# One pipeline step of a fused attention and two-layer kernel, its TensorE order written anew

## The chip, the cores and the metric

The kernel runs on one core of a Trainium2 chip. Its time is the device time of one execution in microseconds (us); of several executions the median counts. Before the change three executions took 552.87, 554.39 and 555.17 us, so the median is 554.39 us.

A core has five engines that run their own queues in order and meet only through semaphores: TensorE (PE in the profile, with PEld for its weight loads), VectorE (DVE), ScalarE (ACT), GpSimd (POOL) and SyncE (SP, which here issues the transfers).

## The reference, cut to what matters

```python
# q, k, v: batch 2, heads 8, sequence 768, head size 64; n_global 8, n_local 96
scores = q @ k.T / 8 - slope[h] * dist            # local band and a few global columns are kept
a = softmax(scores);  x = a @ v                   # x: 1536 tokens x 512
h = x @ w_in                                      # 1536 x 1024
s = h * softmax(h)
ln = (s - mean(s)) / sqrt(var(s) + 1e-6) * g_ln
y = ln @ w_out                                    # 1536 x 512
xn = y / sqrt(mean(y*y) + 1e-6) * rms_g
g, val = xn @ w_gate, xn @ w_val                  # 512 -> 1536 each
out = (g * sigmoid(g) * val) @ w_out2             # 1536 x 512
```

Everything is in 32 bit. The large matmuls are made of three products each: an operand is split into a high part and a low part (`hi`, `lo`), and hi·hi, hi·lo and lo·hi are added up in PSUM.

## The kernel before, in words

The 1536 tokens are cut into 12 units of 128 tokens. A unit goes through the first three layers (attention, `w_in` with its softmax and layer norm, `w_out` with its root mean square); that is phase 1. Phase 2, some 60% of the time, takes the normalised units in groups of four through the gated layer.

Phase 1 is a software pipeline. Its first part is an order written out by hand (`START`), which also converts the weights. From the fifth unit on, `slot(u)` runs once for each u from 4 to 10: seven slots. Six of them hold the full set of work; the last has no scores left to do. One slot works on five units at once:

- `up` for unit u: 2 x 12 matmuls of 512 columns into the banks `h` (line 475), then a maximum on DVE (line 483).
- `p_t` and `attend` for unit u+1: the softmax rows are transposed on PE (line 318, bank `t`), copied to SBUF by ACT or DVE (lines 326 and 328), and multiplied with v (line 340, bank `x`). Each of the four steps does two heads. `x_evac` then splits the result into `xhi` (ACT) and `xlo` (DVE, line 358), which the next slot's `up` reads.
- `scores` for unit u+2, in two halves of four heads: the matmul (line 265, 64 rows of the array for each head), the maximum with the bias on DVE (line 280), the exponential on ACT (line 291), and the division on POOL (line 302).
- `soln` for unit u: the softmax of h on ACT and DVE (lines 497 to 528), which frees the two `h` banks when its products (line 507) are done.
- `ln_t` for unit u-2: the result is transposed on PE (line 542) and split into `lhi` (ACT) and `llo` (DVE, line 226).
- `down` for unit u-3, in four parts of 6 matmuls into the single bank `d` (line 560). After the last part `rms` squares it on ACT (line 573), takes the power on POOL (line 577) and scales it on DVE (line 579, `xn`), which frees the bank.
- `xn_t` for unit u-4: its `xn` is transposed on PE (line 589) and split into `xgh` (ACT) and `xgl` (DVE).

The order on PE in a slot is the order of the calls in `slot`. The orders of ACT, DVE, POOL and SP in the slots are set by the framework's own scheduler, which works from the same calls; so a new order of calls moves these queues too. PSUM has eight banks: two each for `h`, `s` and `t`, one each for `x` and `d`. A tile that asks for a bank waits until its former tile has been read for the last time. The `t` banks are shared in turn by `p_t`, `ln_t` and `xn_t`.

Of the kernel before, what the change touches and what calls it, by code (L numbers as in the profile page):

```python
# [25 lines left out]
NU = B * NB  # L26
# [3 lines left out]
KF = FF // P  # L30
# [12 lines left out]
LEAD = 1  # L43
LAG = 2
DLAG = 3
# [50 lines left out]
w_lo 14 vector, s_exp 5 0, so_mean 2, s_norm 5 0, s_max 5 1, ln_t 1 0  # L96
ln_t 1 1, so_mul 3 0, so_mean 3, s_exp 5 1, s_norm 5 1, w_lo 15 vector
so_var 3, down 0 2, w_mul 12 none, w_mul 14 none, down 0 3, so_var 2"""
N_START = 4
ORDER = [b * NB + j for j in range(NB) for b in range(B)]  # L100
EPS = 1.0e-6
# [19 lines left out]
class Kernel:  # L121
# [127 lines left out]
        )  # L249
        self.v[i] = t  # L250

    def scores(self, u, hh):
        self.s_mm(u, hh)
        self.s_max(u, hh)
        self.s_exp(u, hh)
        self.s_norm(u, hh)
# [488 lines left out]
    def phase1(self):  # L745
# [4 lines left out]
        with self.tc.manual_schedule(engines={E.PE}):  # L750
            for u in range(N_START, NU - LEAD):
                self.slot(u)

    def slot(self, u):

        a = u + LEAD
        s = a + 1
        if s < NU:
            self.load_unit(s)
        if u < NU:  # L760
            self.up(u, 0)
        if a < NU:
            self.p_t(a, 0)
            self.p_t(a, 1)
        if u < NU:
            self.up(u, 1)
        if a < NU:
            self.attend(a, 0)
            self.attend(a, 1)
            self.p_t(a, 2)  # L770
            self.p_t(a, 3)
        if s < NU:
            self.scores(s, 0)
        else:
            self.ln_t(u - LAG, 0, "s")
        if a < NU:
            self.attend(a, 2)
            self.attend(a, 3)
            self.x_evac(a)
        if s < NU:  # L780
            self.ln_t(u - LAG, 0)
        self.ln_t(u - LAG, 1)
        if s < NU:
            self.scores(s, 1)
        if u < NU:
            self.soln(u)
        if u > DLAG:
            self.xn_t(u - DLAG - 1, "t" if s < NU else "s")
        if u >= DLAG:
            for part in range(KF // 2):  # L790
                self.down(u - DLAG, part)

    def phase2(self, w1x, w2x):
        tc, E = self.tc, mybir.EngineType
# [310 lines left out]
```

## Time and profile before

| what | value |
|---|---|
| median of three executions | 554.39 us |
| the profiled execution | 552.96 us, of it 551.1 us between its first and last instruction (the span) |
| PE busy | 526.2 us (95% of the span) |
| PEld, DVE, ACT, POOL busy | 77%, 61%, 43%, 33% |
| mean granted clock of TensorE | 0.991 of full speed |
| chain of work that ended last | PE 78%, DVE 14%, POOL 3%, ACT 2% of the span |

How to read it: a busy share says how much of the span an engine worked, not what the others waited for. Matmuls overlap, so the time from the start of one to the start of the next (the step) is what a matmul costs; the profile's duration of one is longer. So the pace of PE is read from the starts of its instructions, not from its busy time. What is in brackets at the end of a row is idle time of the engine and who ended it.

### The profile page before, as it was taken

To read this page: it belongs to the slowest core of one execution; us is meant where nothing else is said; L and a number is where in the kernel's file an instruction comes from. 1 tells how busy PE (TensorE), PEld (TensorE's weight loads), DVE (VectorE), ACT (ScalarE), POOL (GpSimd) and SP (SyncE) were. 2 spreads that over 40 slices of the span, in tenths; PEclk is the share of its full clock that TensorE was granted. 3 is DMA by queue.
4 is the path that set the end of the run, shared out by engine and by line. 5 is a ranking of instruction groups with operands and counts; after the bars stand their busy time and mean duration, and the time that the engine had idled before them with its cause. 6 is when DMAs were issued, how large, how long until landed. Compare 5 with 4: busy or idle time off the path is not lost.

```text
span 551.1 us, 7636 instructions
## 1 busy us (share of the span) xinstructions
PE 526.2 (95%) x2736; PEld 424.2 (77%) x2736; DVE 338.5 (61%) x797; ACT 235.2 (43%) x557; POOL 179.2 (33%) x207
## 2 busy tenths in 40 slices
PE   4789989999999999999999999999999999999995
PEld 3456767778777888888888888888888888888883
DVE  6989999775577567984725556565654574331312
ACT  5678767664574465643422333422222223111110
POOL 4885253312330331323611332532332232211010
PEclk9979999999999999999999999999999999999999
DMA  8764612330231021340402122222111211020202
GB/s 289 252 231 153 243 47 68 96 96 24 73 97 39 1 77 41 114 152 1 152 2 76 40 76 96 96 78 76 54 62 39 75 40 39 0 77 0 77 0 83
DMA packets 16669, 45.92 MB, mean 83 GB/s; under 512 B 1904, under 2 KB 2928, under 8 KB 16624
## 3 DMA queue, kind: packets, MB, share of 16 engines
q1 hardware_dynamic: 16624, 45.36, 24.3%
q8 instruction: 23, 0.38, 0.3%
q14 instruction: 22, 0.18, 0.1%
HBM read 42.21 MB, written 3.15 MB: 82 GB/s over the span
## 4 chain that ended last, share of the span: by engine, by line
PE 78%; DVE 14%; POOL 3%; ACT 2%; DMA 1%; issue 1%; SPq 0%; POOLq 0%; DVEq 0%; ACTq 0%
PE gv L634 36%; PE op L658 17%; PE yp L560 11%; PE hp L475 9%; DVE p L280 3%; POOL p L302 2%; DVE e L507 2%; PE tp L318 2%; PE xps L340 1%; DVE hst L483 1%; PE tp L589 1%; DVE xlo L358 1%; DVE llo L226 1%; DMA wsh<-in_w_in 1%; DVE pT L328 1%
## 5 line engine op out<-in xcount | busy, mean ns | idle before, releaser
L634 PE MATMUL gv<-xgh,w2hi 128*128 128x512 f32 x288 | 112.2, 390 | 0.0
L634 PE MATMUL gv<-xgl,w2hi 128*128 128x512 f32 x288 | 112.1, 389 | 0.0
L634 PE MATMUL gv<-xgh,w2lo 128*128 128x512 f32 x288 | 112.0, 389 | 0.0
L226 POOL TENSOR_TENSOR alo<-th,ahi 128x512 fp32r<-128x512 f32 x36 | 46.7, 1297 | 199.7 <-ACT ahi L225 199.7
L302 POOL TENSOR_SCALAR p<-p,ast 128x256 f32<-128x256 f32 (+1 forms) x96 | 57.8, 619 | 103.0 <-DVE ast L284 67.5
L475 PE MATMUL hp<-win,xhi 128*128 128x512 f32 x192 | 66.0, 407 | 0.7 <-ACT xhi L220 0.7
L225 ACT ACTIVATE ahi<-th 128x512 fp32r<-128x512 f32 x36 | 22.8, 632 | 98.2 <-DVE th L622 98.2
L620 ACT ACTIVATE th<-gv 128x512 f32<-128x512 f32 x36 | 21.5, 596 | 98.5 <-PE gv L634 98.5
L634 PEld LDWEIGHTS gv<-xgh,w2lo 128*128 128x128 f32 x288 | 54.1, 188 | 11.3
L634 PEld LDWEIGHTS gv<-xgh,w2hi 128*128 128x128 f32 x288 | 54.1, 188 | 11.1
L634 PEld LDWEIGHTS gv<-xgl,w2hi 128*128 128x128 f32 x288 | 54.1, 188 | 11.1
L560 PE MATMUL yp<-wout,lhi 128*128 128x512 f32 x192 | 60.9, 398 | 0.3 <-DVE wout L458 0.3
L621 DVE SCALAR_TENSOR_TENSOR th<-th,gv 128x512 f32<-128x512 f32 x36 | 24.7, 687 | 58.1 <-ACT th L620 58.1
L226 POOL TENSOR_TENSOR w2lo<-wc,w2hi 128x512 fp32r<-128x512 f32 x36 | 49.7, 1384 | 29.6 <-ACT w2hi L225 29.6
L658 PE MATMUL op<-w2hi,alo 128*128 128x512 f32 x144 | 56.0, 389 | 0.0
L658 PE MATMUL op<-w2lo,ahi 128*128 128x512 f32 x144 | 56.0, 389 | 0.0
L658 PE MATMUL op<-w2hi,ahi 128*128 128x512 f32 x144 | 56.0, 389 | 0.0
L622 DVE SCALAR_TENSOR_TENSOR th<-th,gv 128x512 f32<-128x512 f32 x36 | 24.7, 687 | 42.9 <-PE gv L634 42.7
L291 ACT ACTIVATE p<-p,ast 128x256 f32<-128x256 f32 (+1 forms) x96 | 45.9, 480 | 7.1 <-DVE ast L284 3.9
L392 DVE TENSOR_SCALAR wc<-wc 128x512 uint32<-128x512 uint32 x36 | 22.4, 626 | 39.9 <-ACT wc L220 39.8
L475 PEld LDWEIGHTS hp<-win,xhi 128*128 128x128 f32 x192 | 37.1, 193 | 9.3 <-ACT xhi L220 1.4
L394 DVE SCALAR_TENSOR_TENSOR wc<-ws,wc 128x512 uint32<-128x512 uint32 x36 | 40.4, 1123 | 1.1
(118 smaller groups left out, 921.5 us busy)
## 6 DMA issues: line engine op xcount, KB each, us to landing
ws<-in_w SPq DMA_DIRECT2D x36, 512.0 KB, 3.3
qk<-in_qk SPq DMA_DIRECT2D x20, 384.0 KB, 4.0
v<-in_v SPq DMA_DIRECT2D x10, 512.0 KB, 4.1
out_dram<-acc SPq DMA_DIRECT2D x12, 256.0 KB, 2.4
wsh<-in_w_in SPq DMA_DIRECT2D x4, 512.0 KB, 5.4
wsl<-in_w_in SPq DMA_DIRECT2D x4, 512.0 KB, 6.0
wsh<-in_w_out SPq DMA_DIRECT2D x4, 512.0 KB, 4.0
wsl<-in_w_out SPq DMA_DIRECT2D x4, 512.0 KB, 4.8
```

The lines of the kernel that those rows point to most:

```text
L225: self.nc.scalar.activation(out=hi, in_=src, func=AF.Copy)
L226: lo_eng.tensor_tensor(lo, src, f32(hi), ALU.subtract)
L291: self.nc.scalar.activation(out=pt[:, i, 0:W], in_=pt[:, i, 0:W], func=AF.Exp, scale=0.125, bias=st[:, 1, i:i + 1], accum_out=st[:, 2, i:i ...
L302: nc.gpsimd.tensor_scalar(pt[:, i, 0:W], pt[:, i, 0:W], st[:, 3, i:i + 1], 0.0, ALU.mult, ALU.add)
L392: nc.vector.tensor_scalar(w, w, 3, None, ALU.logical_shift_left)
L394: nc.vector.scalar_tensor_tensor(out=w, in0=low, scalar=29, in1=w, op0=ALU.logical_shift_right, op1=ALU.bitwise_or)
L475: nc.tensor.matmul(hp, a[:, k, :], self.win[w][:, k, c], start=(n == 0), stop=(n == len(mms) - 1))
L560: nc.tensor.matmul(yp, a[:, k, :], self.wout[w][:, k, :], start=(k == 0 and n == 0), stop=(k == KF - 1 and n == 2),)
L621: nc.vector.scalar_tensor_tensor(out=a, in0=a, scalar=1.0, in1=g, op0=ALU.add, op1=ALU.mult)
L622: nc.vector.scalar_tensor_tensor(out=a, in0=a, scalar=0.5, in1=v, op0=ALU.mult, op1=ALU.mult)
L634: nc.tensor.matmul(pp, w[:, c], a[:, k, :], start=(n == 0), stop=(n == 3 * KD - 1))
L658: nc.tensor.matmul(self.ops[t], a[:, c], w[:, c0], start=(first and n == 0), stop=(last and n == 2))
```

## The change

`slot` is written as a table, `SLOT`, of 23 steps, and a short loop that calls them. The same steps run on the same units; what differs is their order, and the PSUM bank of the second half of the scores, which is now one of the `h` banks (`scores 1 h`) instead of `s`.

```diff
+SLOT = """\
+up 0, load_unit, p_t 0, p_t 1, up 1, p_t 2, p_t 3, down 0, attend 0, attend 2, attend 1, soln, attend 3,
+ln_t 0 t, scores 0 s, scores 1 h, down 1, down 2, x_evac, xn_t, ln_t 1, down 3"""
...
-    def scores(self, u, hh):
-        self.s_mm(u, hh)
+    def scores(self, u, hh, bank="s"):
+        self.s_mm(u, hh, bank)
...
-        a = u + LEAD
-        s = a + 1
-        if s < NU:
-            self.load_unit(s)
-        if u < NU:
-            self.up(u, 0)
-        if a < NU:
-            self.p_t(a, 0)
-            self.p_t(a, 1)
-        if u < NU:
-            self.up(u, 1)
-        if a < NU:
-            self.attend(a, 0)
-            self.attend(a, 1)
-            self.p_t(a, 2)
-            self.p_t(a, 3)
-        if s < NU:
-            self.scores(s, 0)
-        else:
-            self.ln_t(u - LAG, 0, "s")
-        if a < NU:
-            self.attend(a, 2)
-            self.attend(a, 3)
-            self.x_evac(a)
-        if s < NU:
-            self.ln_t(u - LAG, 0)
-        self.ln_t(u - LAG, 1)
-        if s < NU:
-            self.scores(s, 1)
-        if u < NU:
-            self.soln(u)
-        if u > DLAG:
-            self.xn_t(u - DLAG - 1, "t" if s < NU else "s")
-        if u >= DLAG:
-            for part in range(KF // 2):
-                self.down(u - DLAG, part)
+        unit = dict(up_mm=u, up_max=u, soln=u, p_t=u + LEAD, attend=u + LEAD, x_evac=u + LEAD,
+                    load_unit=u + LEAD + 1, scores=u + LEAD + 1, ln_t=u - LAG, down=u - DLAG,
+                    up=u, xn_t=u - DLAG - 1)
+        for step in SLOT.split(","):
+            name, *args = step.split()
+            i = unit[name]
+            if i < NU and (i >= 0 or name not in ("down", "xn_t")):
+                if u + LEAD + 1 >= NU and (name == "xn_t" or step.split()[:2] == ["ln_t", "0"]):
+                    args = args[:name == "ln_t"] + ["s"]
+                getattr(self, name)(i, *(int(x) if x.isdigit() else x for x in args))
```

On PE, in a full slot, from the last matmuls of the second `up` on. Names: hp is `up`, xps the product with v, tp a transpose (of p, e or xn), sA and sB the scores, yp is `down`. Before:

```order
L475 MATMUL hp<-win_131,xhi 128x512 x4
L340 MATMUL xps<-pT,v 64x128 x8
L318 MATMUL tp<-ident,p 128x128 x8
L265 MATMUL sA<-qk 128x256
L265 MATMUL sB<-qk 128x256
...
L340 MATMUL xps<-pT,v 64x128 x8
L542 MATMUL tp<-ident,e 128x128 x8
L265 MATMUL sA<-qk 128x256
...
L589 MATMUL tp<-ident,xn 128x128 x4
L560 MATMUL yp<-wout_132,lhi 128x512
```

After the last row shown stand the other 23 matmuls of `down`, and then the next slot. The same place of the changed kernel, where all lines are 3 higher:

```order
L478 MATMUL hp<-win_131,xhi 128x512 x4
L321 MATMUL tp<-ident,p 128x128 x8
L563 MATMUL yp<-wout_132,lhi 128x512
...
L343 MATMUL xps<-pT,v 64x128 x16
L545 MATMUL tp<-ident,e 128x128 x4
L268 MATMUL sA<-qk 128x256
L268 MATMUL sB<-qk 128x256
...
L563 MATMUL yp<-wout_132,lhi 128x512
...
L592 MATMUL tp<-ident,xn 128x128 x4
L545 MATMUL tp<-ident,e 128x128 x4
```

The two runs of products with v are one run of 16, the two runs of scores are one of 8 (each counts twice in the trace, where a 32 bit matmul shows as two), the transposes of p stand between `up` and the first 6 matmuls of `down`, and the rest of `down` is cut into runs of 12 and 6.

On ACT, one full slot, from the square of the last `down` (sq<-yp) on: pT copies, the exponentials of h (e<-hp), of the scores (p<-p), the square of the centred e (sq<-e), and the high parts xhi, lhi, xgh. Before:

```order
L573 ACTIVATE sq,rst<-yp 128x512
L326 ACTIVATE pT<-tp 128x512
L500 ACTIVATE e,hst<-hp,hst 128x512
...
L220 ACTIVATE xhi<-xps 128x512
L225 ACTIVATE lhi<-tp 128x512 x2
L291 ACTIVATE p,ast<-p,ast 128x256 x4
L225 ACTIVATE xgh_1252<-tp 128x4x128
L291 ACTIVATE p,ast<-p,ast 128x256 x4
L524 ACTIVATE sq,hst<-e 128x1024
```

and in the changed kernel:

```order
L576 ACTIVATE sq,rst<-yp 128x512
L329 ACTIVATE pT<-tp 128x512 x2
L503 ACTIVATE e,hst<-hp,hst 128x512 x2
L527 ACTIVATE sq,hst<-e 128x1024
L228 ACTIVATE lhi<-tp 128x512
L223 ACTIVATE xhi<-xps 128x512
L294 ACTIVATE p,ast<-p,ast 128x256 x8
L228 ACTIVATE xgh_1264<-tp 128x4x128
L228 ACTIVATE lhi<-tp 128x512
```

The square of e moved from the end of the slot to a place ahead of `lhi` and of all score exponentials, the eight score exponentials stand in one run, and `xgh` and the second `lhi` stand behind them.

## Rows read from the trace of the kernel before

**Rows 1.** Stretches: length, then busy us of PE, PEld, DVE, ACT, POOL, clock.

```profile
86.67:106.94 20.27, 19.46 (x127) 15.24 (x126) 18.10 (x67) 14.82 (x42) 7.54 (x15) 1.00 0.23 73
106.94:201.43 94.49, 93.77 (x621) 75.31 (x620) 61.43 (x216) 52.81 (x150) 23.98 (x46) 1.00 0.19 59
201.43:218.10 16.67, 16.56 (x109) 13.56 (x108) 11.37 (x27) 7.64 (x17) 1.63 (x4) 1.00 0.00 1
218.10:551.10 333.00, 326.31 (x1461) 269.83 (x1459) 170.32 (x239) 98.11 (x175) 98.38 (x77) 1.00 0.19 64
```

**Rows 2.** Timeline of one full slot on PE: start us, us, instruction.

```profile
125.86 0.39 PE L475 MATMUL hp<-win,xhi 128*128 128x512 f32 x1
...
128.59 1.03 PE L318 MATMUL tp<-ident,p 128*128 128x128 f32 x8
129.38 0.48 PE L475 MATMUL hp<-win,xhi 128*128 128x512 f32 x1
...
132.29 1.09 PE L340 MATMUL xps<-pT,v 128*64 128x128 f32 x16
...
134.34 0.48 PE L265 MATMUL sA<-qk 64*128 64x256 f32 x1
...
134.66 0.38 PE L265 MATMUL sA<-qk 64*128 64x256 f32 x1
...
134.87 0.38 PE L265 MATMUL sA<-qk 64*128 64x256 f32 x1
...
135.40 1.09 PE L340 MATMUL xps<-pT,v 128*64 128x128 f32 x16
136.42 1.09 PE L542 MATMUL tp<-ident,e 128*128 128x128 f32 x8
137.45 0.48 PE L265 MATMUL sA<-qk 64*128 64x256 f32 x1
```

**Rows 3.** Timeline of all engines behind the second scores, first and third slot.

```profile
100.95 0.42 PEld L589 LDWEIGHTS tp<-ident,xn 128*128 128x128 f32 x4 [0.88 <-DVE llo L226]
...
138.79 0.42 PEld L589 LDWEIGHTS tp<-ident,xn 128*128 128x128 f32 x4 [0.54 <-DVE llo L226]
...
139.20 0.71 PE L560 MATMUL yp<-wout,lhi 128*128 128x512 f32 x2
```

**Rows 4.** Timeline on PE in the first part, where 32 products stand together.

```profile
62.17 1.97 PE L340 MATMUL xps<-pT,v 128*64 128x128 f32 x32
64.07 1.09 PE L542 MATMUL tp<-ident,e 128*128 128x128 f32 x8
...
65.84 0.38 PE L265 MATMUL sA<-qk 64*128 64x256 f32 x1
...
66.17 0.49 PE L475 MATMUL hp<-win,xhi 128*128 128x512 f32 x1
```

**Rows 5.** Groups in one full slot, by shape: count, busy us, mean ns, idle before.

```profile
L291 ACT ACTIVATE p<-p,ast 128x256 f32<-128x256 f32 x8 | 4.0, 498 | 0.5 <-DVE hst L525 0.4
L280 DVE CUSTOM_DVE_ANT_0 p<-sB,bias 128x256 f32<-128x256 f32 x4 | 1.7, 418 | 0.0
L500 ACT ACTIVATE e<-hp,hst 128x512 f32<-128x512 f32 x2 | 1.4, 690 | 3.5 <-DVE hst L497 3.5
L226 DVE TENSOR_TENSOR llo<-tp,lhi 128x512 fp32r<-128x512 f32 x2 | 1.3, 680 | 0.0
L524 ACT ACTIVATE sq<-e 128x1024 bf16<-128x1024 f32 x1 | 1.0, 1042 | 0.0
L579 DVE SCALAR_TENSOR_TENSOR xn<-yp,rst,rms_bc 128x512 f32<-128x512 f32 x1 | 0.8, 750 | 0.7 <-POOL rst L577 0.7
```

**Rows 6.** Timeline of POOL in one full slot.

```profile
141.14 2.42 POOL L302 TENSOR_SCALAR p<-p,ast 128x256 f32<-128x256 f32 x4 [13.51 <-DVE ast L284]
143.98 1.84 POOL L302 TENSOR_SCALAR p<-p,ast 128x256 f32<-128x256 f32 x4 [0.43 <-DVE ast L300]
145.99 0.55 POOL L577 TENSOR_TENSOR rst<-rst,neghalf 128x1 f32<-128x1 f32 x1 [0.17 <-DVE rst L574]
```

## The prediction

> **What bounds the kernel now.** I first cut the span into stretches. The six full slots run from 86.67 to 201.43 us; the last five of them take 94.49 us, 18.90 each, and PE is busy in 93.77 of these, at a clock of 1.00 [rows 1]. DVE has 61.43 of work there, ACT 52.81, POOL 23.98, so each has room, and what stands on PE is the time. Behind the slots come 333.00 us with PE busy in 326.31 [rows 1]; a time saved ahead of that stretch is saved at the end, if its start finds the converted weights ready, and nothing in the change alters how many there are to convert.
>
> Then I read PE's timeline of one slot, for the starts of runs and not for durations. Twelve matmuls of `up` take 2.73 us (125.86 to 128.59), .227 each [rows 2]. The other runs cost more than their steps, since each change of kind costs something at its ends: eight transposes take .79 between two runs of `up` (128.59 to 129.38), but 1.03 between products with v and scores (136.42 to 137.45) [rows 2]. Four scores take 1.06 (134.34 to 135.40) the first time and 1.34 the second (137.45 to 138.79), where PE's weight load for `xn_t` waits for `llo` on DVE [rows 2, 3]. That wait is the only one of PE that I see in a slot; the rest is pace.
>
> **The change part by part.** The work on PE is the same, instruction for instruction; I price its new runs from these rows, per full slot.
>
> - The wait. `xn_t` needs a `t` bank that the first `ln_t` held until `llo` was done. In the new order the banks are asked for by four p_t, `ln_t 0`, `xn_t`, `ln_t 1`, so `xn_t` takes the bank of the fourth p_t, copied some eight us before. What is late next is `ln_t 1`, which needs the first `llo`; I put that some two us ahead of its need. Saved: 1.34 - 1.06 = .28.
> - Products with v: 1.02 twice (135.40 to 136.42 [rows 2]) become one run of 32, which the first part of the program has too: 62.17 to 64.07, 1.90 [rows 4]. Saved: .14.
> - The second p_t pair stands between matmuls of 512 columns now: .79 for 1.03. Saved: .24. (1.03 is 132.29 to 134.34 less one run of products.)
> - The second four scores follow the first with the step of .21 (134.66 to 134.87 [rows 2]): .84 for 1.06. Saved: .22. The step from scores to a 512-column matmul is in no full slot; in the first part it took .33 (65.84 to 66.17 [rows 4]), against .32 from scores to products (134.87 + .21 to 135.40). Cost .01; bounds: .1 less, if nothing has to be changed, and .2 more, twice the surplus of the runs above.
> - `down` in three runs of 6, 12 and 6. The run behind `xn_t` takes 139.20 to 144.76 (125.86 + 18.90), 5.56 for 24 x .227 = 5.45, so a run's start costs .11 [rows 2, 3]. Two starts more cost .22. The change to products with v, .07 (129.38 to 132.29 is 2.91: 2.73 + .11 + .07), is paid as before.
> - `ln_t` in halves. One half with `xn_t`, between 512-column runs, costs .79; the other 1.03 less four transposes of .10, .63. Before it was 1.03 and, for `xn_t`, .41 (138.79 to 139.20 [rows 3]). Saved: .02.
>
> Sum: .28 + .14 + .24 + .22 - .01 - .22 + .02 = .67, a slot of 18.23. As a cross-check, the new slot in its order, `up`, p_t, `up`, p_t, `down` 6, products, `ln_t`, scores, `down` 12, transposes, `down` 6: 2.73 + .79 + 2.84 + .79 + 1.54 + 1.90 + .63 + 1.90 + 2.84 + .79 + 1.47 = 18.22.
>
> What must hide. Everything else moves off PE, and its cover is now thinner.
>
> - The borrowed `h` bank: the second scores wait for the second product of `soln`. `up` ends at 6.4 of a slot, and maximum, a small instruction, two exponentials and the product (.68 + .2 + 1.38 + .68 [rows 5]) end near 9.6, or 9.9 with hand-overs; the second scores are due at 12.2. Without that cover each us costs one us a slot, since the whole rest of PE's queue stands behind.
> - The single `d` bank: `down 0` comes at 7.1 now, and not at 13.3 (139.20 - 125.86), and needs `xn` of the `down` before.
> - That `xn` closes a ring without PE. DVE works in order: behind `xn` two maxima of `up` with a copy between them; then exponentials on ACT, products, the mean, the square on ACT that now stands ahead of `lhi`; `llo`; and only behind `llo` the maxima of the scores; then eight exponentials in a row, the last four divisions on POOL, and behind them the power for the next `xn`. Durations [rows 5, 6]: .75 + 3 x .68 + 2 x .69 + .68 + .75 + 1.04 + .69 + .68 + 5 x .42 + 8 x .50 + 1.84 + .55 = 16.5 (where no row has the shape, the nearest of the same engine). Some twelve hand-overs come on top; POOL's rows show .17 and .43 of idle time at two, others overlap. At .05 each the ring takes 17.1 us, at .2 it takes 18.9. I take .1, 17.7: the small waits are nearer to .17 than the rows' .43, and DVE's durations overlap, which a sum of them counts twice. That is half a us under 18.22. Before, the ring had PE in it and `xn` came long before it was asked for.
>
> POOL's prices could move with DVE's. In the slot shown four divisions took 2.42 the first time and 1.84 the second: one of them was .58 longer, while DVE subtracted the mean from SBUF to SBUF [rows 6]. The Trainium skill, page SBUF — State Buffer, section Who interferes with whom, says that GpSimd shares a port pair with VectorE and that a VectorE instruction with at most one SBUF input, outside its two-port modes, does not contend for it. By that rule the new neighbours of the divisions, `xgl` and `llo`, which read one operand from PSUM, cost them nothing, and the mean now runs while POOL is idle. If rather any large DVE instruction stretched a division, the ring would grow by .58 for each.
>
> Total: six full slots x .67 = 4.0; in the first of them the wait was longer by .88 - .54 = .34 [rows 3]; the seventh slot has no scores, keeps about .1 of these savings by price, and up to .7 if its waits go too: I take .5. That is 4.9, rounded to 5. The profiled execution took 552.96 us, so 548.0. It is 1.43 under the median; the same saving from 554.39 gives 549.4, my forecast.
>
> **The rivals.**
>
> - The ring decides a little: hand-overs nearer to .15, a ring of 18.5. Then PE waits .3 in most slots, at a transpose that needs a `t` bank or at `down 0`: 5 - 6 x .3 = 3.2, 551.2. For it: half a us is thin in a sum of twenty terms. Against it: in this trace most of these engines' instructions follow each other at once.
> - The change doesn't do what it says: the cost of a change of kind moves to the new places (start of `down` three times, scores to `down` at the upper bound), and only the waits go. 7 x .28 + .34 = 2.3: 552.1. For it: two of the new changes have no row in a full slot. Against it: the long run of products and the transposes at .79 have theirs.
> - Slower: divisions on POOL stretched by DVE. At 17.7 + .58 k the ring passes the present slot of 18.90 with k = 3; from there the kernel is slower. With k = 3, 19.44, it loses .54 in six slots, 3.2: 557.6; with all eight, 22.3 and 575. For it: the .58 of this trace; against it: the other seven divisions of the slot were not stretched, one of them beside `xgl`.
> - The start of the last stretch finds weights late, since the conversions of the last slot stand elsewhere in ACT's and DVE's queues: one loss of 0 to 3, which leaves 549 to 552.
>
> **How the numbers follow.** Forecast .64; the ring decides a little .16; only the waits .10; slower .06; late weights .04. Under .5% (2.8 us, about what a measurement can tell from no change) lies the border at 551.6. All of the forecast's own range, 547.4 to 550.8 (each full slot between .45 and 1.0), is on the faster side, and most of the first rival and half of late weights: .64 + .11 + .02 = .77. Within .5%: the rest of these and the second rival, .17, of which I give .02 to slower for what I don't see: .15 and .08. The range reaches down to 547.0, where a slot saves nearly 1.1, and up to 552.5, so that it holds the ring's case and the second rival; beyond it are the slower case and parts of the others.
>
> **What the profile after would show.** Full slots of 18.2; one run of products of 1.90; scores to `down` in .3 to .4; no idle time of the weight load at `xn_t`; `xn` done some 5 us into a slot, two before `down 0`. The ring would show as idle time of PE at the first transposes of p behind `llo` or `xgl`, or at `down 0` behind `xn`, and as a second maximum of `up` that starts at once behind the copy and not behind PE. A stretched division shows as over 2 us for four. I am wrong if the slots are as long as before, if PE idles at the borrowed bank behind the products of `soln`, or if the saving is there at 201 us and gone at 260.

## The result, and the profile after

The changed kernel takes 548.98 us (median of 6 runs, 548.07 to 551.18), the kernel before 553.60 beside it (6 runs, 552.01 to 555.17): a ratio of 0.9917, 95% interval 0.9896 to 0.9939. It is faster by 4.6 us, 0.8%; 549.4 was forecast, in 547.0 to 552.5. Its profiled execution took 548.55 us with a span of 546.7, against 552.96 and 551.1.

The table has 22 steps, as many as the slot before had calls. All lines of the code after it are three further down: L592 transposes `xn`, L563 is `down`, L229 makes `llo` and `xgl`, L268 the scores.

The span of after in stretches, with the columns of [rows 1]: first full slot, five more, the seventh, the hand-over to the first `gate_val`, and all behind the slots.

```profile
86.27:105.62 19.35, 19.00 (x128) 15.33 (x126) 16.47 (x63) 13.03 (x37) 4.67 (x10) 1.00 0.21 73
105.62:196.62 91.00, 91.00 (x622) 75.11 (x620) 62.97 (x215) 51.55 (x152) 21.12 (x46) 1.00 0.19 62
196.62:212.70 16.08, 16.08 (x110) 13.54 (x108) 13.18 (x31) 10.57 (x25) 5.05 (x10) 1.00 0.11 34
212.70:238.62 25.92, 24.91 (x128) 20.32 (x126) 23.60 (x46) 14.42 (x30) 8.94 (x8) 1.00 0.41 142
212.70:546.70 334.00, 326.75 (x1461) 269.83 (x1459) 169.96 (x239) 97.01 (x173) 97.52 (x76) 1.00 0.18 62
```

Five full slots take 91.00 us, 18.20 each, and PE is busy in all of it; before it was 94.49 [rows 1], 18.90. The first saves .93, the five 3.49, the seventh .59: 5.0. But the stretch behind the slots has become 1.00 longer with the same work (334.00 for 333.00 [rows 1]), although its last part happened to be .42 shorter. The hand-over alone is where it went: this is the line of the kernel before.

```profile
218.10:242.60 24.51, 24.51 (x127) 20.31 (x126) 21.77 (x41) 15.42 (x32) 9.78 (x9) 1.00 0.39 140
```

From 24.51 to 25.92 is 1.41, and PE idles in 1.01 of it. So the span's -4.4 is made of -5.0 in the slots, +1.4 at the hand-over, and -.40 and -.42 at the two ends, which belong to no part of the change: the first part of the program, unchanged, ended at 86.27 here and at 88.58 in another execution of the same kernel.

PE's timeline of one full slot of after, to be read for the starts of runs, as [rows 2] were.

```profile
126.54 1.03 PE L321 MATMUL tp<-ident,p 128*128 128x128 f32 x8
127.33 0.48 PE L478 MATMUL hp<-win,xhi 128*128 128x512 f32 x1
...
130.16 1.03 PE L321 MATMUL tp<-ident,p 128*128 128x128 f32 x8
130.95 0.71 PE L563 MATMUL yp<-wout,lhi 128*128 128x512 f32 x2
...
132.50 1.97 PE L343 MATMUL xps<-pT,v 128*64 128x128 f32 x32
134.39 0.66 PE L545 MATMUL tp<-ident,e 128*128 128x128 f32 x4
134.98 0.48 PE L268 MATMUL sA<-qk 64*128 64x256 f32 x1
...
136.59 0.38 PE L268 MATMUL sA<-qk 64*128 64x256 f32 x1
...
136.91 0.73 PE L563 MATMUL yp<-wout,lhi 128*128 128x512 f32 x2
...
139.77 0.60 PE L592 MATMUL tp<-ident,xn 128*128 128x128 f32 x4
```

Both pairs of p_t take .79, the 32 products 1.90 (132.50 to 134.39), the eight scores 1.93, the step from the last score to `down` .32, and no row has a wait in brackets: the .54 of [rows 3] is gone. Run by run this is the list of the prediction's cross-check, each within .05.

VectorE in the same slot, at the second maximum of `up` (L486).

```profile
127.73 0.75 DVE L582 SCALAR_TENSOR_TENSOR xn<-yp,rst,rms_bc 128x512 f32<-128x512 f32 x1 [1.00 <-POOL rst L580]
...
130.35 0.69 DVE L486 TENSOR_REDUCE hst<-hp 128x1 f32<-128x512 f32 x1 [0.68 <-PE hp L478]
```

`xn` is written 3.9 to 4.7 us into the slot, 2.5 before `down 0` at 7.13, and the second maximum waits .68 for PE and not behind the copy (.67 or .68 in four of the five slots, .22 in the first): in this order the ring does not decide. Eight divisions on GpSimd follow each other in 3.81 us, .48 each, though `xgl` (125.25) and `llo` (125.86) run beside them: the stretch of .58 of [rows 6] is not there. The port rule that the prediction took from the Trainium skill (SBUF — State Buffer, Who interferes with whom) agrees with that here.

Now the hand-over. PE, ScalarE and VectorE of after, from the time at which unit 11's products of `soln` are done (225.2).

```profile
232.00 0.66 PE L592 MATMUL tp<-ident,xn 128*128 128x128 f32 x4 [0.53 <-DVE xn L582]
...
233.60 0.50 PE L563 MATMUL yp<-wout,llo 128*128 128x512 f32 x1 [0.48 <-DVE llo L229]
```

```profile
225.83 0.67 ACT L223 ACTIVATE wc<-ws 128x512 f32<-128x512 f32 x1 [1.17 <-DMA ws<-in_w]
...
227.65 1.06 ACT L527 ACTIVATE sq<-e 128x1024 bf16<-128x1024 f32 x1 [0.68 <-DVE e L519]
...
228.71 0.65 ACT L223 ACTIVATE wc<-ws 128x512 f32<-128x512 f32 x1
229.26 0.58 ACT L576 ACTIVATE sq<-yp 128x512 bf16<-128x512 f32 x1
```

```profile
226.53 0.43 DVE L395 TENSOR_SCALAR wc<-wc 128x512 uint32<-128x512 uint32 x1 [0.29 <-ACT wc L223]
226.87 0.75 DVE L519 TENSOR_SCALAR e<-e,hst 128x1024 f32<-128x1024 f32 x1
...
231.19 0.75 DVE L582 SCALAR_TENSOR_TENSOR xn<-yp,rst,rms_bc 128x512 f32<-128x512 f32 x1 [0.45 <-POOL rst L580]
231.86 1.08 DVE L401 SCALAR_TENSOR_TENSOR wc<-ws,wc 128x512 uint32<-128x512 uint32 x1
232.87 1.27 DVE L229 TENSOR_TENSOR llo<-tp,lhi 128x512 fp32r<-128x512 f32 x2
```

Read it from PE backwards. The transposes of `xn` (unit 8) wait for `xn`, which waits for the square of `yp` on ScalarE (229.26); `yp` had been done since 225.0. That square stands behind two scalings of weight pieces (`wc<-ws`) and behind unit 11's square, which waited for unit 11's mean on VectorE (226.87). The mean stands in VectorE's queue behind L395 of the sixth piece of the second stage's weights; that waits for ScalarE's scaling, and that for a transfer. It is one piece further on than before: in the changed program the scheduler begins with the conversions 8.6 us ahead of the slots' end, where it was 6.9, and each later piece stands one place nearer to the front. The second wait on PE has the same form: `llo` behind L401 of the next piece.

The late transfer is the smaller part of it. These are unit 11's second maximum and its mean in the kernel before, and then the maximum of after.

```profile
224.84 0.68 DVE L483 TENSOR_REDUCE hst<-hp 128x1 f32<-128x512 f32 x1
...
230.78 0.74 DVE L516 TENSOR_SCALAR e<-e,hst 128x1024 f32<-128x1024 f32 x1
```

```profile
220.55 0.68 DVE L486 TENSOR_REDUCE hst<-hp 128x1 f32<-128x512 f32 x1
```

Counted from the end of the slots (218.10 and 212.70), the mean comes at 14.17 us, where it came at 12.68. Of these 1.49, 1.11 are there already at the maximum (7.85 for 6.74), since VectorE works on the third and fourth pieces ahead of it, for whose transfers nothing waited. The other .38 comes with L395 of the sixth, and its idle time is .29.

### The profile page after: what moved, and what is told of

Its sections match the earlier page's. It is cut to its first block, busy times and chain, and to the rows that moved or that the text cites. A ratio compares the mean times of both kernels' runs of the same rounds, so it can differ in the third digit from the quotient of the medians.

```text
span 546.7 us, 7640 instructions
## 1 busy us (share of the span) xinstructions
PE 523.4 (96%) x2736; PEld 424.3 (78%) x2736; DVE 339.4 (62%) x797; ACT 233.9 (43%) x557; POOL 176.1 (32%) x207
## 4 chain that ended last, share of the span: by engine, by line
PE 82%; DVE 10%; POOL 3%; DMA 1%; ACT 1%; issue 1%; POOLq 0%; ACTq 0%; SPq 0%; DVEq 0%
PE gv L637 36%; PE op L661 18%; PE yp L563 9%; PE hp L478 8%; PE xps L343 3%; PE tp L321 3%; POOL p L305 2%; PE sA L268 2%; DVE p L283 2%; PE tp L545 1%; DMA ws<-in_w 1%; PE tp L592 1%; DVE llo L229 1%; DVE wout L461 1%; DVE e L510 1%
## 5 line engine op out<-in xcount | busy, mean ns | idle before, releaser
L229 POOL TENSOR_TENSOR alo<-th,ahi 128x512 fp32r<-128x512 f32 x36 | 46.7, 1297 | 200.5 <-ACT ahi L228 200.5
L305 POOL TENSOR_SCALAR p<-p,ast 128x256 f32<-128x256 f32 (+1 forms) x96 | 54.5, 585 | 105.8 <-ACT p L294 80.6
L563 PE MATMUL yp<-wout,lhi 128*128 128x512 f32 x192 | 62.4, 405 | 0.4 <-DVE wout L461 0.4
L229 POOL TENSOR_TENSOR w2lo<-wc,w2hi 128x512 fp32r<-128x512 f32 x36 | 49.6, 1383 | 23.9 <-ACT w2hi L228 23.9
L395 DVE TENSOR_SCALAR wc<-wc 128x512 uint32<-128x512 uint32 x36 | 22.9, 635 | 40.3 <-ACT wc L223 40.2
```

Of the source, the lines that this page charges most:

```text
L229: lo_eng.tensor_tensor(lo, src, f32(hi), ALU.subtract)
L305: nc.gpsimd.tensor_scalar(pt[:, i, 0:W], pt[:, i, 0:W], st[:, 3, i:i + 1], 0.0, ALU.mult, ALU.add)
L395: nc.vector.tensor_scalar(w, w, 3, None, ALU.logical_shift_left)
L563: nc.tensor.matmul(yp, a[:, k, :], self.wout[w][:, k, :], start=(k == 0 and n == 0), stop=(k == KF - 1 and n == 2),)
```

## The experiments

The letter that a text gives a theory holds in that text. Slot lengths are the mean of the five full slots, from stretches as above.

**The same again.** To tell an accident of one execution from the order of the queues: no edit.

> The changed kernel itself, run again. In its first profile the seven slots saved 5.0 us on PE, but at the hand-over to the second phase PE lost 1.4 us in two waits, behind a weight transfer that landed 5.05 us after its issue where others take about 3.1. Theory A (chance): the late landing is not part of the change; in this profile full slots are 18.20 again, the landing takes about 3.1, the two waits are gone, and the span is 545 to 546. Theory B (the new order of the queues causes it): the same two waits of about 1.4 together, span 546.5 to 547.5.

549.38 us (median of 4 runs, 549.11 to 551.10), a ratio of 0.9909 (0.9879 to 0.9939). Full slots of 18.20, the late landing again (4.9 us), and the two waits of the hand-over again (the two runs of 12 `down` matmuls took 3.43 and 3.60 us, where 2.83 and 2.88 were before). The waits are no accident. The span of 549.3 lies above both texts: this profile is of the slowest of the four, and its slots begin 2.3 us later (88.58 for 86.27).

**The wait of `xn_t` alone.** The kernel before, with one bank changed; the order on every engine stays.

```
-            self.xn_t(u - DLAG - 1, "t" if s < NU else "s")
+            self.xn_t(u - DLAG - 1, "h" if s < NU else "s")
```

> The kernel before, with one edit: the transposes of xn take a bank of h and not of t, so that they need not wait for llo; the order on every engine stays. Theory A (pace of runs and one wait): only the wait goes, .28 in a full slot and .62 in the first, so full slots are 18.62 and the time is 2.0 less, 551.0 against 552.96. Rival (the wait was all that counted, the joined runs are worth nothing): full slots fall to 18.2 or near, the time by over 4.

551.55 us in one run. Its slots, and its second scores on PE:

```profile
106.63:200.12 93.49, 93.49 (x621) 75.30 (x620) 62.22 (x216) 53.06 (x152) 24.38 (x47) 1.00 0.19 60
```

```profile
136.92 0.48 PE L265 MATMUL sA<-qk 64*128 64x256 f32 x1
137.00 0.48 PE L265 MATMUL sB<-qk 64*128 64x256 f32 x1
...
138.06 0.66 PE L589 MATMUL tp<-ident,xn 128*128 128x128 f32 x4
```

Slots of 18.70, .20 less and not .28; the first slot is .52 shorter and not .62. The second scores take 1.14, not the 1.06 of the first: `sB` starts .08 behind `sA`, where it is .01 at the first scores. VectorE's last maximum of the first four ends at 136.94, just ahead of `sB`. So a small wait for bank `s` was hidden under the larger one, and it is gone only with the borrowed bank. The hand-over takes 24.52 as before: its queues are those of before.

**Products cut in two again.** The changed kernel, with

```
-up 0, load_unit, p_t 0, p_t 1, up 1, p_t 2, p_t 3, down 0, attend 0, attend 2, attend 1, soln, attend 3,
+up 0, load_unit, p_t 0, p_t 1, up 1, attend 0, attend 1, p_t 2, p_t 3, down 0, attend 2, soln, attend 3,
```

> The changed kernel with the products with v cut into two runs of 16 again, the second p_t pair and down 0 between them; all else in its order. Theory A: one change of kind more on either side of a run, 2.91 + 1.02 + .85 + 1.54 + 1.02 = 7.34 where the changed kernel has 7.07, so full slots of 18.47 and 1.9 us more in seven slots. Rival (joining is worth nothing): full slots stay at 18.20.

**Scores cut in two again.**

```
-ln_t 0 t, scores 0 s, scores 1 h, down 1, down 2, x_evac, xn_t, ln_t 1, down 3"""
+scores 0 s, ln_t 0 t, scores 1 h, down 1, down 2, x_evac, xn_t, ln_t 1, down 3"""
```

> The changed kernel with the first ln_t between the two halves of the scores, so the scores are two runs of 8 rows again, and products are followed by scores at once, a change of kind that no trace has shown. Theory A: the second start of scores costs .22, full slots of 18.4 if products to scores costs about .2 as products to transposes and transposes to scores do; 18.2 if that direct change is free. Rival: joining scores is worth nothing and full slots are 18.2 or less.

552.82 and 550.11 us, one run each; here are the full slots of the products' kernel, then those of the scores'.

```profile
106.73:199.27 92.53, 92.53 (x621) 74.68 (x620) 62.65 (x215) 51.97 (x153) 21.31 (x47) 1.00 0.18 61
```

```profile
106.25:198.35 92.10, 92.10 (x621) 74.68 (x620) 62.31 (x215) 51.82 (x150) 21.28 (x46) 1.00 0.18 61
```

18.51 and 18.42, where theory A gave 18.47 and 18.4: the joined products and the better place of the second p_t pair are worth .31 a slot, the joined scores .22. It is pace, for no row of PE there has a wait in brackets, and `sB` starts within .01 of `sA`. (In the first kernel the hand-over takes 2.7 us more than before the change, which is why its time says more than its slots.) In the second the scores follow the products directly, and the price is the same as with transposes between:

```profile
133.35 1.97 PE L343 MATMUL xps<-pT,v 128*64 128x128 f32 x32
135.25 0.48 PE L268 MATMUL sA<-qk 64*128 64x256 f32 x1
```

1.90 again. The Trainium skill (TensorEngine Tiling (Array Packing), Tiling Modes) says that a change of the tiling mode drains TensorE. The rows agree in part: 128*64 products and 64*128 scores pay at their ends (16 products take 1.02 us and 32 take 1.90, so .14 of a run doesn't grow with it). But the first matmul of `up` behind the transposes takes .32 to the next (127.33 to 127.65), where .23 is the step, and both are 128*128. So not all of what a change of kind costs is one of mode.

**The borrowed bank.** The changed kernel with `scores 1 s` for `scores 1 h` in its table.

> The changed kernel with the second scores in bank s instead of the borrowed h. Theory A (PE reaches the second scores 1.0 us after the first, and s is read out by then only if VectorE has done its maxima, which it does 2 to 3 us after the scores): PE waits some 2.2 us in each full slot at the second scores, the slot is 20.4 and the time 549 + 6.5 x 2.2 = some 563. Rival (the borrowed banks are of no use, since two s buffers are there): slots stay at 18.20 and the time at 549.

571.79 us in one run, more than either text gave. In each full slot PE waits 1.97 us at the second scores (2.11 in the first). But the slots differ: the second to the fifth take 22.3 to 23.8 us at a mean granted clock of .86 to .92, and the sixth is this one.

```profile
199.52:220.32 20.80, 18.83 (x125) 15.25 (x124) 12.93 (x44) 10.41 (x30) 2.89 (x7) 1.00 0.14 51
```

PE at the second scores of the fifth (22.37 us), and two stretches behind them:

```profile
189.08 0.38 PE L268 MATMUL sB<-qk 64*128 64x256 f32 x1
191.43 0.70 PE L268 MATMUL sA<-qk 64*128 64x256 f32 x2 [1.97 <-DVE ast L283]
...
194.05 1.05 PE L563 MATMUL yp<-wout,lhi 128*128 128x512 f32 x2
...
195.32 1.06 PE L563 MATMUL yp<-wout,lhi 128*128 128x512 f32 x2
```

```profile
191.43:192.83 1.40, 1.40 (x8) 0.99 (x8) 1.20 (x5) 0.34 (x1) 0.00 (x0) 1.00 0.00 0
192.83:197.27 4.44, 4.44 (x13) 3.45 (x13) 2.10 (x13) 3.70 (x16) 1.97 (x5) 0.62 0.00 0
```

The wait is there as theory A had it, 2.35 less the step of .21, until the third maximum has read `sA`. The four scores behind it take 1.40 for .96, each behind a maximum of its bank. 2.14 + .44 is the 2.6 by which the sixth slot exceeds 18.20; theory A's 20.4 lacks only the .44. In the fifth slot the clock comes on top: the 12 `down` matmuls behind the scores take 4.44 us for 2.86, at a mean granted clock of .62. Three of them stand 1.27 apart (194.05 to 195.32) for .68, which is the level of 1.2 and not of 2.4 GHz. These 1.6 us are what 22.37 exceeds 20.80 by.

**A longer ring.** The changed kernel with one line more:

```
+        nc.scalar.activation(out=sq, in_=e, func=AF.Square, accum_out=c(11))
```

> The changed kernel with unit's 128x1024 square on ScalarE done twice (1.06 us and an accumulator read more in each slot; the result is unused). Theory A (ring of VectorE, ScalarE and GpSimd 17.5 us, 0.7 under the slot): the ring becomes 18.7 to 18.9 and decides, PE waits 0.5 to 0.8 us in each full slot, at the transposes of p behind llo or at the second maximum, slots of 18.7 to 19.0, time 552 to 554. Rival (ScalarE and VectorE, idle a third of the slot, have several us to spare): slots stay at 18.20 and the time at 549.

551.96 us in one run. Its last four full slots, then VectorE at the score maxima, at `llo` and at the second maximum of `up`, and PE at the transposes of p (lines behind the edit are one further down):

```profile
125.78:198.88 73.11, 73.11 (x497) 60.06 (x496) 50.21 (x172) 45.30 (x130) 16.83 (x37) 1.00 0.18 59
```

```profile
138.98 0.42 DVE L283 CUSTOM_DVE_ANT_0 p<-sA,bias 128x256 f32<-128x256 f32 x1
...
139.89 0.41 DVE L283 CUSTOM_DVE_ANT_0 p<-sA,bias 128x256 f32<-128x256 f32 x1
...
146.45 0.68 DVE L229 TENSOR_TENSOR llo<-tp,lhi 128x512 fp32r<-128x512 f32 x1
...
150.69 0.69 DVE L486 TENSOR_REDUCE hst<-hp 128x1 f32<-128x512 f32 x1 [0.18 <-PE hp L478]
```

```profile
146.81 1.10 PE L321 MATMUL tp<-ident,p 128*128 128x128 f32 x8
147.66 0.48 PE L478 MATMUL hp<-win,xhi 128*128 128x512 f32 x1
```

Neither text was right, because the dose was not what I took it for: the scheduler set the second square behind `lhi`, where it runs beside the maxima. It holds up two small instructions of VectorE among them (L531, L532), and the third maximum comes .91 behind the first where it was .69 in after. These slots take 18.28 on average, 18.27 in the last three; the full slot ahead of them takes 18.48. That is .6 of the 3.4 us by which the span is longer (550.1); 1.7 stand ahead of these slots and 1.0 at the hand-over (26.92).

What decided is not the ring. PE pays at the transposes of p, .85 for .79 (146.81 to 147.66), a place that the prediction named: they need the bank that `llo` reads. But the second maximum of `up`, which the prediction named too, still waits for PE, .18 for the .68 in after, so the ring without PE had room left. The path that decided starts at PE's second `up` and runs through the maximum, the exponentials, the products and on to `llo`. In after `llo` ends as the transposes start (125.86 + .68, and 126.54); here it ends .32 later than that, and they take .06 more. In the slot of 18.48 it ends .45 later and they take .98; in the first of after's five .24 later, and they take .79. So this path had some .26 of room, an estimate from these few slots.

**The pieces moved behind.** For the hand-over: the sixth piece and the first three after it are queued behind `lhi` and `llo` of unit 10.

```
+                    if i == 1:
+                        behind = self.last
+                        self.load_w2(1, (2,), behind)
...
-                self.load_w2(1)
+                self.load_w2(1, (0, 1))
...
-                self.load_w2(n)
+                self.load_w2(n, behind=behind if n == 2 else ())
```

`self.last` holds ScalarE's and VectorE's instruction of the last `split`, and `load_w2` queues its own behind them, in order of issue only. (The lines of `load_w2` and `split` that do it are left out here; lines between them are one further down.)

> The changed kernel; of the second stage's weights, the sixth conversion piece and the first three after it are queued on ScalarE and VectorE behind lhi and llo of unit 10, where the sixth stood ahead of unit 11's mean before. The slots are untouched. Theory B (the hand-over loses 1.4 us because the mean and the squares of units 11 and 8 stand in VectorE's and ScalarE's queues behind a piece whose transfer has not landed): both waits go, the two runs of 12 down matmuls take 2.83 and 2.88 us again instead of 3.5 and 3.6, the first gate_val starts 1.4 us earlier after the slots' end (24.5 instead of 25.9), the span is 545.3 and the time 547.5 (546.7 to 548.3). Rival (the hand-over is bounded by another chain, for instance PE's own results through ScalarE, and the piece only filled its idle time): the waits stay within 0.3 us of 1.4 and the time stays at 549.

> The changed kernel again, beside the one with the pieces moved, on the same chip. Both theories: slots of 18.20, the hand-over with its two waits (some 1.4 to 1.6 us together), 549.0 (548.1 to 550.0).

The hand-over of the kernel with the pieces moved, and its VectorE there:

```profile
212.98:237.42 24.44, 24.44 (x127) 20.48 (x126) 21.85 (x42) 13.98 (x29) 8.59 (x8) 1.00 0.34 108
```

```profile
226.49 0.75 DVE L520 TENSOR_SCALAR e<-e,hst 128x1024 f32<-128x1024 f32 x1
...
230.01 0.75 DVE L583 SCALAR_TENSOR_TENSOR xn<-yp,rst,rms_bc 128x512 f32<-128x512 f32 x1 [0.67 <-POOL rst L581]
230.68 1.28 DVE L229 TENSOR_TENSOR llo<-tp,lhi 128x512 fp32r<-128x512 f32 x2
```

And that of the changed kernel beside it:

```profile
212.47:238.26 25.79, 24.92 (x127) 20.31 (x126) 23.65 (x46) 14.42 (x30) 8.96 (x8) 1.00 0.44 142
```

24.44 for 25.79: both waits are gone, with slots of 18.20 in both. The mean now follows the small instruction ahead of it at once, `xn` and `llo` come first and the pieces behind them (from 231.88). A transfer landed late here too, in 4.8 us. So it is the queues' order that made the loss; a late landing alone makes none. The time shows less of it: 548.58 us (547.68 to 550.09, 6 runs; ratio 0.9902, 0.9879 to 0.9925) for 548.92 (548.03 to 551.64, 6 runs; 0.9919, 0.9893 to 0.9946). The intervals overlap, and my 547.5, in 546.7 to 548.3, was too low: in the two profiles the moved pieces' kernel starts its slots .50 later and takes .44 longer behind the hand-over, at the ends that differ between executions anyway. This version is ahead of both others in the profile; against the changed kernel the times leave it open.

## Why the prediction was right

- *The slots.* 18.23 was forecast, 18.20 came, with all rows that were named. Within the sum some sizes were off. The wait was .20 and not .28 (the kernel with one bank changed); the rest of the 1.34 was a wait for bank `s` under it, which went too, so that .28 + .22 - .01 for the scores became .47 (2.40 for all eight to 1.93). Products and p_t pair, .38 in the sum, are that by the rows of after too (2.04 to 1.90 and 1.03 to .79); the kernel that cuts the products sets the p_t pair in another place than before, so its .31 doesn't undo just these two.
- *Starts of `down`.* -.22 forecast. The three runs exceed 24 x .227 by .19, .14 and .10 (1.55, 2.86, 1.46 us) and `up 1` by .10, .53 together; before it was .29 (.18 of 2.91, .11 of 5.56): -.24.
- *First and seventh slot.* 1.01 and .5 forecast, .93 and .59 measured.
- *The borrowed bank.* The second product of `soln` is done 9.7 us into the slot and the second scores start at 12.1: no wait, as said. But the price of losing that cover, one us a slot for each us of wait, was too low: 2.1 of wait cost 2.6 in the slot that kept its clock, and 4.1 to 5.6 in the four that did not.
- *The ring.* It didn't decide, and its size was right: the second maximum had .68 of idle time in a slot of 18.20, so the ring took some 17.5, where 17.7 was forecast. What was missed is another path with less room, some .26: from PE's second `up` to `llo` and the bank of the next transposes of p. The prediction had that place only as a sign of the ring.
- *POOL.* No division was stretched in the slot shown, and GpSimd's work in the five slots fell from 23.98 to 21.12; the slower rival had no part in it.
- *The step that failed* is the first: that a time saved ahead of the last stretch is saved at its end, if the stretch finds its weights ready. They were ready: PE goes on to `gate_val` without a wait (238.62). 1.41 of the 5.0 was given back all the same, by pieces of later weights that stand in VectorE's and ScalarE's queues ahead of what `down` still needs from the last units. The rival of late weights had the place and, within its 0 to 3, the size, at a chance of .04, and the queues too; but it was not the weights that came late, it was the work behind their conversion.
- *The number.* 5.0 saved, less 1.4, and .8 that the two ends of the program gave in that execution make 4.4 of span; the medians differ by 4.6, and not by 5.0. The base moved as well: 549.4 is 5.0 under 554.39, the median of three executions, and of six it is 553.60. With the loss foreseen the forecast would have been 550.8. So the slots were forecast rightly, and that 549.4 met 548.98 so closely is luck.

## What to carry to other kernels

Where PE is never idle, read the starts of runs: joining the scores paid .22 us a slot here, and joining the products with a better place for a pair of p_t .31, near what the rows had said. But whoever moves work in a loop whose other engines are ordered by a scheduler should compare those engines' queues at the loop's exit too: work that is wanted late, and may wait for a transfer besides, stands there ahead of work that is wanted now. Placing it behind that work by hand gave back all of the 1.4 us at the hand-over; whether the whole time is shorter for it the runs leave open.

## What the runs showed of the hardware

- After a wait of 2 us on PE, in the kernel with bank `s`, the granted clock fell in four of six full slots and stayed at 1.00 in two, the first (88.30 to 108.71 us) and the sixth. Against the sixth (20.80 us) the four took 1.5 to 3.0 us more. In the fifth it was 1.00 through the first 1.40 us after the wait and .62 in the mean of the next 4.44, with matmuls at nearly twice their step in most of these. What tells the slots apart stays open. Waits of .5 us at the hand-over of after left the clock at 1.00.
- One transfer of a weight piece landed later than its neighbours. Issues at 220 to 221 us, with KB each and median us to landing:

```profile
ws<-in_w SPq DMA_DIRECT2D x1, 512.0 KB, 5.0
```

The six issues of 200 to 232 us, this one among them, have a median of 3.2. It was 4.9 us in the repeat, but 3.5 in the kernel with the scores cut, whose hand-over had waits all the same (25.57 us), and 4.8 in the kernel with the pieces moved, whose hand-over had none. So the place in the queues made the waits. Why it lands late stays open.
